# RWKV-7 chunk kernel with an MLP behind it: chunk operations in 64x64 tiles, PSUM banks in pairs, one full-array phase per slot

## The chip, the cores and the metric

The kernel runs on 1 core of one Trainium2 chip. The metric is the device time of one execution in microseconds, the median of three runs. Profiles are of one profiled execution. PE is TensorE, DVE VectorE, ACT ScalarE, POOL GpSimd, and SP the engine whose queue issues most DMAs.

## The reference

An RWKV-7 recurrence over 4 batch rows, 8 heads, 768 steps and a head size of 40, and then an MLP on each of the 3072 tokens:

```python
for t in range(S):
    y[:, :, t] = einsum('bhd,bhde->bhe', rt, state)
    Sa = einsum('bhde,bhe->bhd', state, at)
    state = state * wt[:, :, None, :] - einsum('bhd,bhe->bhde', Sa, bt)
    state = state + einsum('bhd,bhe->bhde', vt, kt)
x = y as (tokens, 320)
h = x @ w_in                                   # 320 -> 1024
solu = h * softmax(h)
ln = (solu - mean) / sqrt(var + 1e-6) * g_ln
out = ln @ w_out                               # 1024 -> 320, w_in, g_ln, w_out in float64
```

## The kernel before

The recurrence is worked in chunks of C = 64 steps. Two batch rows lie on the 128 partitions (64 steps each), so a *slot* i is one chunk of one pair of batch rows: 2 pairs times 12 chunks, N = 24 slots; the two pairs alternate, and the state `st` of a pair is carried from slot i to slot i + 2. A head's product is at most 64 by 64, and the array is used as four tiles of 64x64: `units` lists the 16 (p, g, q, h) of a slot (batch row p and head), and `in_turn` deals them out so that neighbouring instructions lie on different tiles. Other work uses the array as one: the transpositions of 128 rows (`turned`, four transposes of two heads each), the decay sums (`decay`: `pcum`, `pex`), the transposition of the MLP's activations (`folded`: `plnT`), and the two MLP products (`hidden`: `h`, `output`: `po`).

For a slot the steps are these. `load_keys` and `load_values` load w, b, k, a and v, r. `decay` takes the logarithm of w, sums it along time (`pcum`, `pex`), and scales b and k by the inverse decay (`kb`, POOL). `front` writes `kb` to DRAM and turns b and a (`pbT`, `paT`; `bT` is copied by ACT, `aT` is a product by `ex` on DVE). `norm` multiplies them (`pnt`), masks the product (`nt`) and writes it to DRAM. For each group of GRP = 4 slots `spread` gathers the 32x32 diagonal blocks of `nt` in `blk`, and `invert` inverts them on DVE, in 30 pairs of operations (`prod`, `uu`); they come back through DRAM by `bring` (`tu`, `uh`). `couple` and `close` (`py`, `pz`) make the off-diagonal part of the inverse. `fetch` brings `kb` back (`kbx`), `attend` turns k, v and r (`pkT`, `pvT`, `prT`), `states` turns the state (`psT`), `scores` multiplies (`ps`), `carried` and `driven` make the right side (`px`, copied to `x0`), `solved` applies the inverse (`pu`), `answered` (`pl`) and `read` (`pyo`) make the output and the new state, and `leave` scales both and sends the output to `xT`. Then come `hidden`, `weighed`, `spreadof`, `folded` and `output`, one and two slots later.

One Python loop over i from -9 to N + 1 writes all of this as a software pipeline: the step of slot i stands beside `norm` of slot j = i + 7 (AHEAD), `front` of j + 1, `decay` of j + 2 and `load_keys` of j + 3. PE's order is exactly the written one (`manual_schedule`); the orders of the other engines are set by the tile scheduler. `some(n)` takes the next n pairs of the inversion, `drawn(n)` the next n pieces of the weights' conversion from float64 (`narrow`, on DVE, POOL and ACT), which in the kernel before runs nine pieces at each of i = -4 to -1 and the rest at the end of i = 0. PSUM is one tag of six banks of 2 KB a partition (`bank`) and two banks for `h`. `in_value_order` copies v and r on POOL into another order of heads.

Of the kernel before, what the change touches and what calls it, by code (L numbers as in the profile page):

```python
# [45 lines left out]
def kernel(  # L46
# [34 lines left out]
    ps1 = ctx.enter_context(tc.tile_pool(name="ps1", bufs=6, space=PSUM))  # L81
# [32 lines left out]
    r_t = zeroed(nc.gpsimd, "r", [P, H, C], 2, pad)  # L114
    v_t = zeroed(nc.gpsimd, "v", [P, H, C], 2, pad)
# [12 lines left out]
    def bank(name):  # L128
        return ps1.tile([P, 512], FP32, tag="bank", name=name)
# [43 lines left out]
    def weights():  # L173
# [5 lines left out]
        pg = bank("pg")  # L179
# [6 lines left out]
        t = bank("pmean")  # L186
# [13 lines left out]
    units = [(p, g, q, h) for g in range(2) for p in range(2) for q in range(2) for h in range(2)]  # L200
# [16 lines left out]
    def pair(t, j):  # L217
        return t[:, j:j + 2, :].rearrange("p a b -> p (a b)")[:, 0:W2]
# [10 lines left out]
    def load(x, ap, i):  # L229
        bp, ci = where_(i)  # L230
        for p in range(2):
            nc.sync.dma_start(out=x[half(p), :, 0:D],
                              in_=ap[2 * bp + p, :, ci * C:(ci + 1) * C, :].rearrange("h t d -> t h d"))
# [5 lines left out]
    def load_keys(i):  # L239
        if not ok(i):  # L240
            return
        d = st[i]
        for n, ap in (("w", w), ("b", b), ("k", k), ("a", a)):
            x = a_t[i % 3] if n == "a" else two.tile([P, H, D], FP32, tag="raw_" + n, name="raw_" + n)
            d["raw_" + n] = x
            load(x, ap, i)

    def load_values(i):
        if not ok(i):
            return  # L250
        d = st[i]
        for n, ap in (("v", v), ("r", r)):
            d["raw_" + n] = two.tile([P, H, D], FP32, tag="raw_" + n, name="raw_" + n)
            load(d["raw_" + n], ap, i)

    def in_value_order(i):
        if not ok(i):
            return
        d = st[i]
        d["v"], d["r"] = v_t[i % 2], r_t[i % 2]  # L260
        d["lv"] = two.tile([P, H, W2], FP32, tag="lv", name="lv")
        for x, n in ((d["v"][:, :, 0:D], "raw_v"), (d["r"][:, :, 0:D], "raw_r"), (d["lv"][:, :, C:], "raw_v")):
            nc.gpsimd.tensor_copy(out=x.rearrange("p (h x) d -> p h x d", h=2),  # L263
                                  in_=d[n].rearrange("p (x h) d -> p h x d", h=2))


    def decay(i):
# [5 lines left out]
        t = bank("pcum")  # L273
        nc.tensor.matmul(heads(t[:, 0:DM]), lhsT=c_("cum"), rhs=lw[:, :, 0:D], start=True, stop=True)  # L274
        inv = two.tile([P, DM], FP32, tag="inv", name="inv", bufs=1)
        nc.scalar.activation(out=inv, in_=t[:, 0:DM], func=AF.Exp, scale=-1.0)  # L276
        t = bank("pex")
        for j in range(4):
            nc.tensor.matmul(t[0:W2, j * P:(j + 1) * P], lhsT=pair(lw, 2 * j), rhs=c_("cum"), start=True, stop=True)  # L279
        ex = d["ex"] = ex_t[i % (AHEAD + 3)]  # L280
        nc.scalar.activation(out=ex[0:W2, :, :, 1:].rearrange("p b j t -> p j b t"),
                             in_=t[0:W2].rearrange("p (j b t) -> p j b t", j=4, b=2), func=AF.Exp)
# [5 lines left out]
    def turned(name, src_, bufs=1, evict=True):  # L288
        t = bank("p" + name)
        for j in range(4):  # L290
            nc.tensor.transpose(out=t[0:W2, j * P:(j + 1) * P], in_=pair(src_, 2 * j), identity=ident)  # L291
        if not evict:
            return t
        o = two.tile([P, 4, P], FP32, tag=name, name=name, bufs=bufs)
        nc.scalar.copy(out=o[0:W2].rearrange("p j t -> p (j t)"), in_=t[0:W2])
        return o

    def front(i):
        if not ok(i):
            return  # L300
        d = st[i]
        nc.sync.dma_start(out=d["kb_dram"], in_=d["kbw"])
        ex = d["ex"]
        d["bT"] = turned("bT", d["kbw"][:, H:, :])
        t = turned("aT", d["raw_a"], evict=False)
        aT = d["aT"] = two.tile([P, 4, P], FP32, tag="aT", name="aT", bufs=AHEAD + 2)
        nc.vector.tensor_tensor(out=aT[0:W2].rearrange("p j (b t) -> p j b t", b=2),
                                in0=t[0:W2].rearrange("p (j b t) -> p j b t", j=4, b=2),
                                in1=ex[0:W2, :, :, 0:C].rearrange("p b j t -> p j b t"), op=ALU.mult)

    def masked(dst, t):
        nc.vector.tensor_tensor(out=dst, in0=t, in1=tri.unsqueeze(1).to_broadcast([P, 4, C]), op=ALU.mult)  # L312

    def keyed(t, i, u):
        p, g, q, h = u
        return t[rows(h), 2 * g + q, p * C:p * C + C]

    def valued(t, i, u):
        p, g, q, h = u
        return t[rows(q), 2 * h + g, p * C:p * C + C]  # L320

    def norm(i):
# [3 lines left out]
        t = [bank("pnt") for _ in range(2)]  # L326
        for u in in_turn(lambda p, g, q, h: (h, p ^ h)):
            p, g, q, h = u
            j = 2 * g + q
            mm(t[h][half(p ^ h), j * C:j * C + C], keyed(d["bT"], i, u), keyed(d["aT"], i, u))  # L330
        nt = d["nt"] = two.tile([P, 2, 4, C], FP32, tag="nt", name="nt", bufs=AHEAD + 1)
        for h in range(2):
            masked(nt[:, h], t[h][:, 0:256].rearrange("p (j c) -> p j c", j=4))
        d["nt_dram"] = dram.tile([P, H, C], FP32, tag="nt_dram", name="nt_dram", bufs=3)
# [35 lines left out]
    def bring(i):  # L370
# [6 lines left out]
        for x in range(2):  # L377
# [4 lines left out]
            nc.sync.dma_start(out=d["uh"][hi],  # L382
                              in_=uu[at + 16 + 8 * x:at + 24 + 8 * x, :, Q:].rearrange("h s t -> s h t"))

    def fetch(i):
# [3 lines left out]
        d["kb"] = two.tile([P, 2 * H, C], FP32, tag="kbx", name="kbx")  # L389
        nc.sync.dma_start(out=d["kb"], in_=d["kb_dram"])  # L390

    def couple(i):
# [3 lines left out]
        t = [bank("py") for _ in range(2)]  # L396
        for u in in_turn(lambda p, g, q, h: p ^ h):
            p, g, q, h = u
            j, x = 2 * g + q, half(p ^ h)
            mm(t[h][x, j * Q:j * Q + Q], d["nt"][x, h, j], d["tu"][x, 4 * h + j, 0:Q])  # L400
        for h in range(2):
            nc.scalar.activation(out=wy[:, h, :, 0:Q], in_=t[h][:, 0:4 * Q].rearrange("p (j c) -> p j c", j=4),
                                 func=AF.Copy, scale=c_("neg_hi"))

    def close(i):
# [3 lines left out]
        t = [bank("pz") for _ in range(2)]  # L409
        for u in in_turn(lambda p, g, q, h: p ^ h):  # L410
            p, g, q, h = u
            j, x = 2 * g + q, half(p ^ h)
            mm(t[h][x, j * Q:j * Q + Q], wy[x, h, j], d["uh"][x, 4 * h + j])
        for h in range(2):
            nc.scalar.copy(out=d["tu"][:, 4 * h:4 * h + 4, 2 * Q:], in_=t[h][:, 0:4 * Q].rearrange("p (j c) -> p j c", j=4))


    def attend(i):
# [3 lines left out]
        d["kT"] = turned("kT", d["kb"][:, 0:H, :])  # L422
        d["vT"] = turned("vT", d["v"])
        d["rT"] = turned("rT", d["r"], bufs=2)

    def scores(i):
# [3 lines left out]
        t = [bank("ps") for _ in range(2)]  # L430
        for u in in_turn(lambda p, g, q, h: (h, p)):
            p, g, q, h = u
            j = 2 * g + q
            mm(t[h][half(p), j * C:j * C + C], keyed(d["kT"], i, u), keyed(d["aT"], i, u))
        for u in in_turn(lambda p, g, q, h: (q, p)):
            p, g, q, h = u
            j = 4 + 2 * h + g
            mm(t[q][half(p), j * C:j * C + C], valued(d["vT"], i, u), valued(d["rT"], i, u))
        psi = d["psi"] = two.tile([P, 2, 4, C], FP32, tag="psi", name="psi")
        for x in range(2):  # L440
            masked(psi[:, x], t[x][:, 0:256].rearrange("p (j c) -> p j c", j=4))
        for x in range(2):
            masked(d["lv"][:, x::2, 0:C], t[x][:, 256:].rearrange("p (j c) -> p j c", j=4))


    def carried(i):
# [5 lines left out]
        d["px"] = [bank("px") for _ in range(2)]  # L452
        d["opened"] = set()
        if ci:
            for u in in_turn(lambda p, g, q, h: (h, p ^ h)):
                p, g, q, h = u
                j = 2 * g + q
                mm(d["px"][h][half(p ^ h), j * D:j * D + D], keyed(d["aT"], i, u),
                   st_t[bp][rows(h), 4 * p + j, 0:D], start=(h, p ^ h) not in d["opened"], stop=False)
                d["opened"].add((h, p ^ h))  # L460
            fence()

    def driven(i):
# [3 lines left out]
        for u in in_turn(lambda p, g, q, h: (p, p ^ h)):  # L467
            p, g, q, h = u
            j = 2 * g + q
            mm(d["px"][h][half(p ^ h), j * D:j * D + D], d["psi"][half(p), h, j],  # L470
               d["lv"][half(p), 4 * h + 2 * g + q, C:], start=(h, p ^ h) not in d["opened"])
            d["opened"].add((h, p ^ h))
        for h in range(2):
# [261 lines left out]
```

## Time and profile before

| | |
|---|---|
| median of 3 runs | 817.25 us (816.14 to 817.75) |
| the profiled execution | 821.3 us |
| its span | 819.5 us |
| mean granted TensorE clock | 0.863 of full speed |
| PE, DVE, ACT, POOL busy | 644.9, 379.0, 239.8, 168.4 us |
| DMA | 84.31 MB in 224901 packets |

The median is of plain runs; the profiled execution is 4 us longer. About 1.8 us of it lie outside the span. A row of the timeline gives the start, the duration, the engine and the line, the operation with its tiles (out<-in) and shapes, the number of instructions, and in brackets the idle time of the engine ahead of it with what ended it. A PE duration includes the pipeline's tail, so consecutive rows overlap, and the cost of a row is best read from start to start.

### The profile page before, as it was taken

To read this page: it belongs to the slowest core of one execution; us is meant where nothing else is said; L and a number is where in the kernel's file an instruction comes from. 1 tells how busy PE (TensorE), PEld (TensorE's weight loads), DVE (VectorE), ACT (ScalarE), POOL (GpSimd) and SP (SyncE) were. 2 spreads that over 40 slices of the span, in tenths; PEclk is the share of its full clock that TensorE was granted. 3 is DMA by queue.
4 is the path that set the end of the run, shared out by engine and by line. 5 is a ranking of instruction groups with operands and counts; after the bars stand their busy time and mean duration, and the time that the engine had idled before them with its cause. 6 is when DMAs were issued, how large, how long until landed. Compare 5 with 4: busy or idle time off the path is not lost.

```text
span 819.5 us, 26810 instructions
## 1 busy us (share of the span) xinstructions
PE 644.9 (79%) x11545; PEld 480.8 (59%) x11545; DVE 379.0 (46%) x1048; ACT 239.8 (29%) x592; POOL 168.4 (21%) x237
## 2 busy tenths in 40 slices
PE   4505506778989989889889899798997877989894
PEld 3304404657757766667667667676765665666652
DVE  3563572478403692343954228822479133123322
ACT  3323102323324322433234334133321222223121
POOL 6664234313202211221022102301111110000000
PEclk8655756669989989999989999799997789899997
DMA  7546847364464545554625655265422412011000
GB/s 149 145 133 138 204 109 191 64 138 95 96 169 108 111 79 129 155 122 89 146 80 115 152 133 127 49 161 125 97 70 52 120 47 54 23 52 41 15 20 13
DMA packets 224901, 84.31 MB, mean 103 GB/s; under 512 B 206088, under 2 KB 213136, under 8 KB 224016
## 3 DMA queue, kind: packets, MB, share of 16 engines
q1 hardware_dynamic: 220272, 76.12, 40.4%
q10 hardware_dynamic: 4512, 6.48, 2.7%
q8 instruction: 91, 1.49, 0.7%
q14 instruction: 26, 0.21, 0.1%
HBM read 49.53 MB, written 29.10 MB: 96 GB/s over the span
## 4 chain that ended last, share of the span: by engine, by line
PE 46%; DVE 23%; DMA 15%; issue 5%; POOL 5%; ACT 3%; SPq 2%; ACTq 0%; DVEq 0%; POOLq 0%
PE h L592 14%; PE po L642 10%; DMA kbx<-kb_dram 7%; DVE prod L360 5%; DVE uu L362 5%; PE pz L211 3%; PE pyo L211 3%; DVE e L604 3%; DVE nmax L595 3%; PE py L211 3%; DVE bs L612 2%; DMA uu_dram<-uu 2%; PE pu L211 2%; POOL n_s L143 2%; ACT e L598 2%
## 5 line engine op out<-in xcount | busy, mean ns | idle before, releaser
L595 DVE TENSOR_REDUCE nmax<-h 128x1 f32<-128x1024 f32 x24 | 29.4, 1223 | 305.0 <-PE h L592 305.0
L592 PE MATMUL h<-w_in,xT 120*128 120x512 f32 (+1 forms) x288 | 135.8, 622 | 0.0
L642 PE MATMUL po<-w,lnT 128*128 128x320 f32 x384 | 115.4, 456 | 3.9 <-ACT lnT L633 3.9
L642 PEld LDWEIGHTS po<-w,lnT 128*128 128x128 f32 x384 | 75.7, 203 | 34.9 <-ACT lnT L633 5.4
L592 PEld LDWEIGHTS h<-w_in,xT 120*128 120x128 f32 (+1 forms) x288 | 55.0, 197 | 62.2 <-issue 61.1
L598 ACT ACTIVATE e<-h,nmax 128x1024 f32<-128x1024 f32 x24 | 26.8, 1116 | 147.5 <-DVE nmax L595 147.5
L360 DVE TENSOR_TENSOR prod<-blk,uu 128x30 f32<-128x30 f32 (+9 forms) x180 | 62.9, 350 | 6.0
L362 DVE TENSOR_TENSOR uu<-uu,prod 128x30 f32<-128x30 f32 (+9 forms) x180 | 61.5, 342 | 5.7
L291 PE MATMUL pkT<-cst,kbx 128*104 128x128 f32 x96 | 18.7, 330 | 45.5 <-DMA kbx<-kb_dram 42.7
L621 POOL TENSOR_TENSOR rs<-c,mhalf 128x1 f32<-128x1 f32 x24 | 13.4, 557 | 188.7 <-DVE c L620 135.6
L285 POOL TENSOR_TENSOR kb<-raw_b,inv 128x320 f32<-128x320 f32 x24 | 20.9, 869 | 151.4 <-ACT inv L276 131.1
L291 PE MATMUL pbT<-cst,kb 128*104 128x128 f32 x96 | 18.4, 323 | 39.5 <-POOL kb L285 39.5
L263 POOL COPY v<-raw_v 128x320 f32<-128x320 f32 x24 | 10.9, 456 | 179.8 <-DMA raw_v<-in_v_dram 179.7
L274 PE MATMUL pcum<-lw,cst 128*128 128x320 f32 x48 | 24.6, 605 | 24.6 <-ACT lw L272 14.7
L211 PE MATMUL pyo<-lv,kbx 64*64 64x104 f32 x768 | 42.2, 268 | 0.5 <-DVE lv L312 0.4
L211 PE MATMUL pyo<-lu,kbx 64*64 64x104 f32 x768 | 41.0, 261 | 0.8 <-DVE lu L312 0.5
L291 PEld LDWEIGHTS pkT<-cst,kbx 128*104 128x104 f32 x96 | 12.2, 154 | 50.0 <-issue 46.9
L644 ACT ACTIVATE osb<-po,rs 128x320 f32<-128x320 f32 x24 | 12.7, 527 | 94.5 <-PE po L642 94.5
L211 PE MATMUL py<-tu,nt 64*64 64x32 f32 x768 | 30.6, 227 | 8.2 <-DMA tu<-uu_dram 6.0
L279 PEld LDWEIGHTS pex<-cst,lw 128*104 128x104 f32 x192 | 32.8, 223 | 7.0 <-issue 4.1
L474 ACT COPY x<-px 128x160 f32<-128x160 f32 x48 | 11.7, 295 | 83.7 <-PE plnT L632 25.4
L291 PEld LDWEIGHTS pbT<-cst,kb 128*104 128x104 f32 x96 | 11.4, 149 | 41.8 <-POOL kb L285 40.5
(105 smaller groups left out, 1253.1 us busy)
## 6 DMA issues: line engine op xcount, KB each, us to landing
kb_dram<-kb SPq DMA_DIRECT2D x24, 512.0 KB
kbx<-kb_dram SPq DMA_DIRECT2D x24, 512.0 KB
nt_dram<-nt SPq DMA_DIRECT2D x24, 256.0 KB
uu_dram<-uu SPq DMA_DIRECT2D x6, 1024.0 KB
raw_w<-in_w_dram SPq DMA_DIRECT2D x48, 80.0 KB
raw_b<-in_b_dram SPq DMA_DIRECT2D x48, 80.0 KB
raw_k<-in_k_dram SPq DMA_DIRECT2D x48, 80.0 KB
a<-in_a_dram SPq DMA_DIRECT2D x48, 80.0 KB
```

Source lines behind the costliest of these rows:

```text
L211: nc.tensor.matmul(o, lhsT=lhsT, rhs=rhs, start=start, stop=stop, skip_group_check=True)
L274: nc.tensor.matmul(heads(t[:, 0:DM]), lhsT=c_("cum"), rhs=lw[:, :, 0:D], start=True, stop=True)
L279: nc.tensor.matmul(t[0:W2, j * P:(j + 1) * P], lhsT=pair(lw, 2 * j), rhs=c_("cum"), start=True, stop=True)
L285: nc.gpsimd.tensor_tensor(out=kb[:, j * H:j * H + H, 0:D], in0=d["raw_" + n], in1=heads(inv), op=ALU.mult)
L291: nc.tensor.transpose(out=t[0:W2, j * P:(j + 1) * P], in_=pair(src_, 2 * j), identity=ident)
L360: nc.vector.tensor_tensor(out=t, in0=nb[:, j:j + 1, j + 1:Q].to_broadcast([P, j, m]), in1=u[:, 0:j, j:j + 1].to_broadcast([P, j, m]), op=A ...
L362: nc.vector.tensor_tensor(out=u[:, 0:j, j + 1:Q], in0=u[:, 0:j, j + 1:Q], in1=t, op=ALU.subtract)
L592: nc.tensor.matmul(h[:, hh], lhsT=d["xT"][0:n, kt, :], rhs=w_in[0:n, kt, hh], start=kt == 0, stop=kt == NK - 1)
L595: nc.vector.tensor_reduce(out=nmax, in_=h, axis=AX.X, op=ALU.max, negate=True)
L598: nc.scalar.activation(out=e, in_=h, func=AF.Exp, bias=nmax, accum_out=d["esum"])
L604: nc.vector.tensor_tensor(out=d["e"], in0=d["h"], in1=d["e"], op=ALU.mult)
L642: nc.tensor.matmul(o[:, 0:DM], lhsT=d["lnT"][:, f, :], rhs=w2[:, f, :], start=f == 0, stop=f == NF - 1)
```

## The change

- The transpositions of k, v, r, a, b and of the state become 16 pieces of 64x64 each (`turn`): a transpose where the result goes to the lower 64 partitions, a matmul by the identity where it goes to the upper ones. `pcum` becomes two products of 64x64 blocks, `pex` sixteen; `py` and `pz` go over four tiles in place of two.
- PSUM's six banks become three pairs (`banks`). k and v share a pair (`pkv`), r and the state another (`prs`), a and b a third (`pa`), the two halves of `plnT` a pair too. One operation evicts both banks: `x0`, `nuT`, `lu`, `wy`, `tu` on ACT, `nt`, `psi`, `lv`, `lu` on DVE.
- The heads keep their natural order: v and r are loaded straight to where they are used, and the POOL copies go. The state's update is two POOL operations in place of one.
- The loop's order: `attend`, `front` and `decay` stand ahead of `solved`; `folded`, `hidden` and `output` are consecutive; `answered`, `scores`, `read` follow. Drains stand ahead of `driven`'s products and ahead of the second half of `read`.
- `nt` is not kept but loaded again from DRAM in `fetch` (`ntx`); `kbx` has three buffers in place of two; `uh` comes in four loads in place of two; k and a of the first four slots are loaded by ACT's queue.
- The weights are converted at i = 0 (20 pieces) and i = 1 (the rest), none before.

```diff
-    def bank(name):
-        return ps1.tile([P, 512], FP32, tag="bank", name=name)
+    def banks(name):
+        return ps1.tile([P, 2, 512], FP32, tag="banks", name=name)
...
-    def turned(name, src_, bufs=1, evict=True):
-        t = bank("p" + name)
-        for j in range(4):
-            nc.tensor.transpose(out=t[0:W2, j * P:(j + 1) * P], in_=pair(src_, 2 * j), identity=ident)
-        if not evict:
-            return t
-        o = two.tile([P, 4, P], FP32, tag=name, name=name, bufs=bufs)
-        nc.scalar.copy(out=o[0:W2].rearrange("p j t -> p (j t)"), in_=t[0:W2])
+    def turn(t, to, of, at, x):
+        o, one = t[half(to), of, at:at + C], ident[half(of), half(of)]
+        if to:
+            mm(o, x, one)
+        else:
+            nc.tensor.transpose(out=o, in_=x, identity=one)
+
+    def turned(t, at, src_, keys):
+        for u in in_turn(lambda p, q, g, h: (p, h if keys else q)):
+            p, q, g, h = u
+            j = at + (2 * q + g if keys else 2 * g + h)
+            turn(t, h if keys else q, p, j * C, src_[half(p), head(u)])
+        return t[0:W2, :, at * C:at * C + 4 * C].rearrange("p b (j t) -> p b j t", j=4)
+
+    def kept(name, t, bufs=1):
+        o = tokens(name, bufs)
+        nc.scalar.copy(out=o[0:W2], in_=t)
         return o
...
     def front(i):
         nc.sync.dma_start(out=d["kb_dram"], in_=d["kbw"])
-        d["bT"] = turned("bT", d["kbw"][:, H:, :])
-        t = turned("aT", d["raw_a"], evict=False)
+        t = banks("pa")
+        a_ = turned(t, 0, d["raw_a"], True)
+        aT = d["aT"] = tokens("aT", AHEAD + 2)
+        nc.vector.tensor_tensor(out=aT[0:W2], in0=a_, in1=d["ex"][0:W2, :, :, 0:C], op=ALU.mult)
+        d["bT"] = kept("bT", turned(t, 4, d["kbw"][:, H:], True))
...
     def attend(i):
-        d["kT"] = turned("kT", d["kb"][:, 0:H, :])
-        d["vT"] = turned("vT", d["v"])
-        d["rT"] = turned("rT", d["r"], bufs=2)
+        t = banks("pkv")
+        d["kT"] = kept("kT", turned(t, 0, d["kb"], True))
+        d["vT"] = kept("vT", turned(t, 4, d["lv"][:, :, C:], False))
+        t = banks("prs")
+        d["rT"] = kept("rT", turned(t, 0, d["r"], False), 2)
+        if ci:
...
+                turn(t, q, h, at, st_t[bp][half(h), 4 * q + 2 * p + g])
+            d["s"] = kept("s", t[0:W2, :, 256:].rearrange("p h (j c) -> p h j c", j=4), 2)
...
     def folded(i):
+        t = banks("plnT")
         for x in range(2):
-            t = bank("plnT")
...
     def fetch(i):
-        d["kb"] = two.tile([P, 2 * H, C], FP32, tag="kbx", name="kbx")
+        d["kb"] = two.tile([P, 2 * H, C], FP32, tag="kbx", name="kbx", bufs=3)
         nc.sync.dma_start(out=d["kb"], in_=d["kb_dram"])
+        d["nt"] = tokens("ntx", 2)
+        nc.sync.dma_start(out=d["nt"].rearrange("p h j c -> p (h j) c"), in_=d["nt_dram"])
...
+        if i == 0:
+            drawn(20)
+        if i == 1:
+            drawn(100)
         carried(i)
         norm(j)
         driven(i)
...
-        in_value_order(i + 1)
-        folded(i - 2)
         attend(i + 1)
+        front(j + 1)
+        decay(j + 2)
         some(3)
         fetch(i + 2)
-        output(i - 2)
         solved(i)
         couple(i + 1)
         some(3)
+        folded(i - 2)
         hidden(i - 1)
-        answered(i)
         weighed(i - 1)
-        scores(i + 1)
+        output(i - 2)
         spreadof(i - 1)
         some(3)
-        front(j + 1)
-        decay(j + 2)
-        states(i + 1)
+        answered(i)
+        scores(i + 1)
         some(3)
-        if -4 <= i < 0:
-            drawn(9)
         read(i, True)
         close(i + 1)
         read(i, False)
         leave(i)
         if (i + 2) % GRP == 0:
             some(40)
-        if i == 0:
-            drawn(100)
         bring(i + 2)
```

## The prediction

> **What bounds the kernel now.** I read the page first, then the windows by stage, then PE's and ACT's timeline of one ordinary slot, then PE's in a late slot. The page gives busy time, the granted clock in 40 slices and the chain that ended last:
>
> ```profile
> PE 644.9 (79%) x11545; PEld 480.8 (59%) x11545; DVE 379.0 (46%) x1048; ACT 239.8 (29%) x592; POOL 168.4 (21%) x237
> PEclk8655756669989989999989999799997789899997
> PE 46%; DVE 23%; DMA 15%; issue 5%; POOL 5%; ACT 3%; SPq 2%; ACTq 0%; DVEq 0%; POOLq 0%
> ```
>
> PE carries the chain but is not the whole of it, and its clock is low for the first eight slices. The windows give, after the stretch, each engine's busy time (PE first) and then the clock:
>
> ```profile
> 0.00:93.00 93.00, 38.94 (x310) 30.55 (x310) 43.60 (x130) 27.47 (x62) 50.01 (x63) 0.63 0.65 150
> 93.00:166.00 73.00, 37.06 (x593) 29.40 (x597) 38.39 (x97) 15.97 (x40) 26.64 (x30) 0.65 0.56 130
> 373.00:482.00 109.00, 97.86 (x1943) 73.64 (x1944) 55.09 (x154) 37.04 (x92) 19.10 (x29) 0.97 0.53 119
> ```
>
> So 166 us pass before slot 1 opens (93 to the first inversion) with PE under half busy. From there four slots take about 109 us, PE 90% busy, clock 0.97. One ordinary slot on PE (start, duration with the pipeline's tail, idle before it in brackets):
>
> ```profile
> 475.23 1.09 PE L632 MATMUL plnT<-cst,e 128*128 128x128 f32 x8
> 476.84 0.62 PE L291 MATMUL pkT<-cst,kbx 128*104 128x128 f32 x4 [0.52 <-DMA kbx<-kb_dram]
> 477.29 0.60 PE L291 MATMUL pvT<-cst,v 128*104 128x128 f32 x4
> 477.73 0.60 PE L291 MATMUL prT<-cst,r 128*104 128x128 f32 x4
> 478.16 4.47 PE L642 MATMUL po<-w,lnT 128*128 128x320 f32 x16
> 482.56 0.69 PE L211 MATMUL pu<-tu,x 64*64 64x64 f32 x32
> 483.52 1.11 PE L211 MATMUL py<-tu,nt 64*64 64x32 f32 x32
> 496.43 1.07 PE L211 MATMUL pz<-uh,wy 64*64 64x32 f32 x28 [0.22 <-DVE c L618]
> ```
>
> Three groups of transpositions run back to back, 0.44 us each, because each has its own bank. Their evictions on ACT trail behind and nobody on PE waits for them:
>
> ```profile
> 477.54 0.59 ACT L295 COPY kT<-pkT 104x512 f32<-104x512 f32 x1 [0.50 <-PE pkT L291]
> 478.02 0.59 ACT L295 COPY vT<-pvT 104x512 f32<-104x512 f32 x1
> 478.50 0.60 ACT L295 COPY rT<-prT 104x512 f32<-104x512 f32 x1
> ```
>
> Late slots instead wait for kbx, and the work after the wait runs at half speed (pkT 1.07 us for 0.62, po 6.02 for 4.47):
>
> ```profile
> 635.51 1.97 PE L632 MATMUL plnT<-cst,e 128*128 128x128 f32 x8
> 639.70 1.07 PE L291 MATMUL pkT<-cst,kbx 128*104 128x128 f32 x4 [2.22 <-DMA kbx<-kb_dram]
> 642.27 6.02 PE L642 MATMUL po<-w,lnT 128*128 128x320 f32 x16
> ```
>
> The sum is made against the profiled execution, 821.3 us (span 819.5 and 1.8 outside). The median is 817.25, so a sum is brought to it by 0.995.
>
> **PE work that goes.** A 64x64 transposition group becomes 8 transposes into columns 0 and 8 matmuls by the identity into columns 64 (two instructions each): 24 instructions over four tiles. Rows of 32 such instructions over four tiles take 0.45 to 0.53 us (pu above to its next group at 483.08: 0.52), so I take 0.45 for a group of 24, as now (0.44): no gain. The bounds are 0.38 and 0.9, the latter if the transposes and the matmuls don't overlap. py and pz use two tiles (1.04 and 1.07 us for 32); over four I take 0.5, the price of the other groups of 32: -1.1. pcum with pex (0.54 and 0.88) become about 1.0: -0.4. The kbx wait of 0.52 goes, since kbx gets a third buffer: -0.5. Two waits of 0.38 and 0.22 ahead of the reading-out are covered by the new order: -0.6. Together -2.6 us in an ordinary slot of 25.3 (px 472.73 to px 498.05).
>
> The phases of full-array work fall from three to one. Between rows I see no stop worth more than 0.1: the last h to pl is 5.36 us for 12 matmuls at 0.443, and the second ps to pbT is 0.58 for its own 0.47. I take 0; the other bound is four changes by 0.11 by 24 slots, -10 us. The Trainium skill, "TensorEngine Tiling (Array Packing)", Key Properties, says that changing the tiling mode drains TensorE, which speaks for the change; it gives no price, and at the row's 0.11 us it is that bound.
>
> **New waits on PE.** Two banks are now one tile, and PE's order is fixed. In the built order the transposes of v, which write the same pair as those of k, wait for ACT's copy of kT; those of st for the copy of rT; those of kb for DVE's aT multiply; the second half of plnT for the first lnT copy. Price of one from the rows: group start to copy start 0.70 (476.84 to 477.54), copy 0.59, start of the next 0.1: 1.39 instead of 0.44, so +0.95. With ACT's x0 copy (0.45) ahead of kT it is 1.15; st 1.1; kb with aT's 0.68 on DVE 1.05; plnT, whose copy stands behind nuT, lu and wy on ACT, 1.4 (0.4 if the scheduler's order let it go first). Together +4.7. Behind each waiting instruction stands all of PE, po and h too. The ordinary slot becomes 25.3 - 2.6 + 4.7 = 27.4 us.
>
> **By groups.** A group from pu to pu is now 25.2, 31.1, 26.1 and 27.1 (109.5). The two long ones after the inversion hold kbx waits, so they become 27.4 as well: +2.2, +1.3, +0.3. The inversion slot changes most in one place: 24 inversion operations (8.2 us by their rows, 390.88 to 399.06) now stand on DVE before aT, and PE's kb transposes wait for it, some 3.4 us later than in other slots; h comes that much later, so nmax, which now waits behind 34 inversion operations, waits less. I take +1.7. That is +5.5 a group, three groups +16.5; slots 13 to 16 +4.7 (105.9 before). From slot 17 on there is no front or decay left: 27.4 less pa, its wait, pb and the decays (3.0) is 24.4, and the kbx waits of 4 to 5 us with their half clock go: slots 17 to 20 take 107 for 117.4, -10.4, and the last ones -3. Sum from slot 1 on: +8, with bounds -30 (half the new waits hidden) and +20.
>
> SP gets a load of nt and two more of uh in each slot, about 1.3 us by their rows; it is done 5 us before its next slot now, which covers them. POOL loses three copies of 0.45, off the path.
>
> **Prologue.** No weight is narrowed before slot 0 any more (nine pieces at each of four steps before), and a norm step takes about 7 us for 8.9, with k and a of the first slots on ACT's queue. The first inversion then starts at 44 to 50 instead of 93. But the narrowing (20 pieces, about 3 us each by POOL's 1.2 to 1.3 and 0.7 to 1.1 a piece and the hops) falls behind it and holds slot 0's and slot 1's evictions and pmean: slot 1 opens near 149, for 166. -17, bounds -30 and +5.
>
> **The clock.** From S+2.85 to S+8 of the new slot (S its px) PE works 1.8 of 5.1 us, in pieces of 0.45. Before's trace shows what idle time does: 1.71 us idle ahead of the plnT at 198.42 was followed by half speed until 201.77; waits of 2 to 3.6 us in inversion and late slots by 4 to 8 us of it; while stretches with up to 43% of 3.4 us idle (the slots at 340 and 367) kept full speed. The new stretch has 65% idle in its worst 3.4 us. Half speed from about S+6.5 to past pu and py would double up to 3 us of PE work. I charge 2.2 us in 12 of 23 slots, +26, with bounds 0 and +60 (2.6 in every slot). The Trainium skill, "TensorE: Matmul & The Clock Gate", Part 1, lets the clock fall after an idle window of some 3.4 us: by that alone none of these stretches counts and the charge is 0, but the row at 198.42 fell after less. Its Part 4 holds that transposes don't count as busy in the same way, by which every slot would fall: +60.
>
> Sum: 821.3 + 8 - 17 + 26 = 838; by 0.995, **834 us**.
>
> **Rivals.** *The clock holds* (faster): the pieces between the waits are enough to keep full speed, as with the 43% windows. 821.3 + 8 - 17 = 812, median 808, and 785 to 812 with the drains saved or waits shorter. It decides at 9 us: fewer than 4 slots charged. For it: the pieces are never more than 1.15 us apart. Against it: 198.42. Chance 0.36. *Transposes and identity matmuls don't share the array* (slower): 0.9 instead of 0.45 us for six groups in 23 slots, +62 less what the waits take up, 860 to 890; no row mixes the two. 0.12. *My forecast, false waits plus the clock*: 0.49, alone 818 to 865. *Nothing measurable*, prologue and waits cancelling: 0.03; 0.2% is about what can be told from no change.
>
> The range takes the faster case from 790 and the slower one up to 880. Faster 0.37, same 0.03, slower 0.60.
>
> **What would show it.** Right: pkv's second half, prs's second, pa's second and plnT's second each with 1 to 1.5 us idle released by ACT kT, rT, DVE aT, ACT lnT; ordinary slots 27 to 30 us; PEclk below 0.9 in the slices from 160 to 590 that read 9 now; kbx gone from the waits; late slots near 24.5; slot 1 at 140 to 155. Wrong: four slots in under 110 us at full clock, a transposition group over 0.7 us at full clock, or slot 1 after 166.

## The result and the profile after

The changed kernel takes 1413.38 us (median of 4 runs, 1408.09 to 1417.93), 1.729 times the kernel before (95% interval 1.722 to 1.736). The forecast was 834 us. Its profiled execution spans 1409.7 us. The page's busy times, the granted clock by slices, and the chain that ended last:

```profile
PE 1210.4 (86%) x15009; PEld 822.3 (58%) x15009; DVE 369.3 (26%) x882; ACT 239.1 (17%) x472; POOL 143.7 (10%) x189
PEclk9655555567577576675775765766756777767779
PE 80%; issue 6%; ACT 4%; DVE 3%; POOL 3%; DMA 2%; ACTq 0%; SPq 0%; DVEq 0%; POOLq 0%
PE pa L211 10%; PE pkv L211 10%; PE h L589 9%; PE prs L211 8%; PE po L639 7%; PE pa L287 6%; PE pkv L287 6%; PE prs L287 5%; PE pyo L211 3%; PE pu L211 3%; PE px L211 2%; PE plnT L629 2%; PE pcum L211 2%; PE ps L211 2%; POOL n_s L143 1%
```

PE's busy time has nearly doubled (644.9 before), and 45% of the span lies on the chain in pa, pkv and prs, the transpositions, which were cheap before. The clock is never back at 9 in the steady part. PE's timeline of one group shows how (L287 is a transpose, L211 the matmul by the identity, two instructions):

```profile
807.42 0.31 PE L287 MATMUL prs<-cst,r 64*64 64x64 f32 x1
807.66 0.47 PE L211 MATMUL prs<-cst,r 64*64 64x64 f32 x2
808.06 0.31 PE L287 MATMUL prs<-cst,r 64*64 64x64 f32 x1
808.30 0.47 PE L211 MATMUL prs<-cst,r 64*64 64x64 f32 x2
...
812.16 0.47 PE L211 MATMUL prs<-cst,r 64*64 64x64 f32 x2
813.40 0.31 PE L287 MATMUL prs<-cst,st 64*64 64x64 f32 x2 [0.77 <-ACT rT L302]
813.64 0.48 PE L211 MATMUL prs<-cst,st 64*64 64x64 f32 x4
814.05 0.32 PE L287 MATMUL prs<-cst,st 64*64 64x64 f32 x2
814.30 0.48 PE L211 MATMUL prs<-cst,st 64*64 64x64 f32 x4
```

Read from start to start. A matmul begins 0.24 us after the transpose ahead of it, and the next transpose 0.24 us after that matmul's second instruction; no other piece starts in between, and no semaphore is waited for. In the state's group, from 813.40 on, two transposes start within 0.01 us of each other, and so do the matmuls behind them: work of one kind does run side by side. The order there is T T M M where the others have T M T M, so it has 8 changes of kind in place of 16, and it takes 2.68 us where the others take 5.2 (medians over the slots). That is 0.33 us a change in either, with the work itself.

The clock follows the groups. In one slot it is full over the MLP and the reading-out, and half over the transpositions, though PE is 92% busy there (stretch, its length, PE, PEld, DVE, ACT, POOL, then the clock):

```profile
774.00:794.00 20.00, 16.96 (x361) 11.79 (x358) 7.72 (x15) 4.81 (x10) 1.42 (x3) 1.00 0.18 62
797.00:827.00 30.00, 27.72 (x148) 17.62 (x149) 0.69 (x1) 2.34 (x4) 0.00 (x0) 0.50 0.41 88
```

The predicted waits are there too, each in nearly every slot (total, times, longest):

```profile
PE pkv L287 <- ACT kT L302: 23.8, 24, 5.6
PE pa L287 <- DVE aT L313: 20.2, 24, 0.9
PE plnT L629 <- ACT lnT L630: 19.7, 24, 1.2
PE prs L287 <- ACT rT L302: 16.8, 22, 0.8
```

They are 80 us of the 590 by which the span grew, and cannot be the cause alone.

### The profile page after: what moved, and what is told of

Its sections match the earlier page's. It is cut to its first block, busy times and chain, and to the rows that moved or that the text cites. A ratio compares the mean times of both kernels' runs of the same rounds, so it can differ in the third digit from the quotient of the medians.

```text
span 1409.7 us, 33414 instructions
## 1 busy us (share of the span) xinstructions
PE 1210.4 (86%) x15009; PEld 822.3 (58%) x15009; DVE 369.3 (26%) x882; ACT 239.1 (17%) x472; POOL 143.7 (10%) x189
## 3 DMA queue, kind: packets, MB, share of 16 engines
q1 hardware_dynamic: 216048, 81.11, 23.6%
## 4 chain that ended last, share of the span: by engine, by line
PE 80%; issue 6%; ACT 4%; DVE 3%; POOL 3%; DMA 2%; ACTq 0%; SPq 0%; DVEq 0%; POOLq 0%
PE pa L211 10%; PE pkv L211 10%; PE h L589 9%; PE prs L211 8%; PE po L639 7%; PE pa L287 6%; PE pkv L287 6%; PE prs L287 5%; PE pyo L211 3%; PE pu L211 3%; PE px L211 2%; PE plnT L629 2%; PE pcum L211 2%; PE ps L211 2%; POOL n_s L143 1%
## 5 line engine op out<-in xcount | busy, mean ns | idle before, releaser
L211 PE MATMUL pkv<-cst,lv 64*64 64x64 f32 x384 | 90.7, 337 | 0.0
L211 PE MATMUL prs<-cst,r 64*64 64x64 f32 x384 | 90.7, 337 | 0.0
L211 PE MATMUL pa<-cst,kb 64*64 64x64 f32 x384 | 90.2, 337 | 0.0
L211 PE MATMUL pa<-cst,a 64*64 64x64 f32 x384 | 89.2, 333 | 0.0
L211 PE MATMUL pkv<-cst,kbx 64*64 64x64 f32 x384 | 85.0, 319 | 0.4 <-issue 0.4
L287 PE MATMUL pkv<-cst,lv 64*64 64x64 f32 x192 | 59.5, 310 | 23.8 <-ACT kT L302 23.8
L287 PE MATMUL pa<-cst,kb 64*64 64x64 f32 x192 | 59.2, 308 | 20.2 <-DVE aT L313 20.2
L287 PE MATMUL pkv<-cst,kbx 64*64 64x64 f32 x192 | 56.7, 295 | 21.1 <-DMA kbx<-kb_dram 19.8
L211 PEld LDWEIGHTS prs<-cst,r 64*64 64x64 f32 x384 | 54.7, 202 | 22.2
L211 PEld LDWEIGHTS pkv<-cst,lv 64*64 64x64 f32 x384 | 54.7, 202 | 22.2
L211 PEld LDWEIGHTS pa<-cst,kb 64*64 64x64 f32 x384 | 54.1, 199 | 22.2
L211 PEld LDWEIGHTS pa<-cst,a 64*64 64x64 f32 x384 | 53.4, 197 | 21.8
L211 PEld LDWEIGHTS pkv<-cst,kbx 64*64 64x64 f32 x384 | 50.6, 186 | 20.6 <-issue 0.5
```

The source lines that it names most:

```text
L211: nc.tensor.matmul(o, lhsT=lhsT, rhs=rhs, start=start, stop=stop, skip_group_check=True)
L287: nc.tensor.transpose(out=o, in_=x, identity=one)
```

## The experiments

**Theory A**: at each change between transposing and multiplying PE waits until the work before it is done. **Rival B**: small pieces of either kind run one at a time. **Rival C**: the prediction's own cause, shared bank pairs and the clock. The first three runs vary only the kind and order of the pieces.

All pieces by matmul:

```diff
-        if to:
-            mm(o, x, one)
-        else:
-            nc.tensor.transpose(out=o, in_=x, identity=one)
+        mm(o, x, one)
```

> Every 64x64 piece of a transposition is a matmul by the identity; none is a transpose. Theory A (each change between transposing and multiplying waits until the array is empty, 0.24 us at half clock, 16 changes a group): a group falls from 5.2 to about 0.5 us, a slot from 55 to 27-30 us, the total to 800-840 us. Rival B (small pieces of either kind run one at a time): 16 matmuls by 0.40 us, 6.4 us a group, the total at 1450 us or more. Rival C (the shared bank pairs and the clock that falls behind them are the cause): the clock stays near 0.68 and the total above 1200 us.

Measured: 905.93 us (896.1 to 906.74), 1.099 of before (1.090 to 1.109). Order, tiles and banks are as in the changed kernel, so they are not the cause. B falls, and C as the main cause: the clock rises to 0.80 and the total is far under 1200. A holds for the 507 us that went, but not for the total of 800 to 840: 85 us are left over the kernel before.

The transposes of a group first, then the matmuls:

```diff
-        for u in in_turn(lambda p, q, g, h: (p, h if keys else q)):
+        lot = in_turn(lambda p, q, g, h: (p, h if keys else q))
+        for u in sorted(lot, key=lambda u: u[3] if keys else u[1]):
...
-            for u in in_turn(lambda p, q, g, h: (h, q)):
+            for u in sorted(in_turn(lambda p, q, g, h: (h, q)), key=lambda u: u[1]):
```

> The same pieces as in the changed kernel, but in each group the 8 transposes come first and then the 8 matmuls: one change inside a group and one between groups in place of 16. Theory A: a group of 0.7 to 1.0 us, the total at 830-890 us. Rival B: 8 x 0.31 us and more remain for the transposes, a group of 3 us or more, the total above 1100 us. Rival C: no change, near 1413 us.

Measured: 960.75 us (957.54 to 966.19). A group takes 1.68 us at half speed, above A's 0.7 to 1.0, and about 1.0 at its fastest. The total is 70 us above A's 890, about what the run before had left over.

T T M M in place of T M T M:

```diff
+        lot = in_turn(lambda p, q, g, h: (p, h if keys else q))
+        for u in [lot[n + k] for n in range(0, 16, 4) for k in (0, 2, 1, 3)]:
```

> Pieces in the order T T M M in place of T M T M, as the state's group already has them: 8 changes a group in place of 16. Theory A: each of five groups falls from 5.2 to 2.7 us, 12.6 us a slot, the total to about 1413 - 24 x 12.6 = 1110 us (somewhat lower with the prologue). Rivals B and C: near 1413 us.

Measured: 1131.22 us (two runs, 1124.55 and 1137.90), all groups 2.3 to 2.7 us. The same pieces, the same banks and the same waits, and half the changes take 282 us off.

The fewer the changes of kind, the shorter the slot. Changes a slot, against the mean of 12 slots from slot 2 on (px to px):

| kernel | changes a slot | us a slot |
|---|---|---|
| changed kernel | 5 x 16 + 8 = 88 | 55.9 |
| T T M M | 6 x 8 = 48 | 42.6 |
| transposes first | 6 x 2 = 12 | 35.8 |
| all matmuls | 0 | 32.3 |
| kernel before | 0 | 27.9 |

From row to row a change costs 0.33, 0.19 and 0.29 us; over all, 23.6 / 88 = 0.27. These prices hold the change of clock as well. No run shows why a change costs this: the trace gives each piece's 64x64 shape, not the mode in which the array runs it.

k, a and b by four transposes of the full array, v, r and the state by matmuls:

```diff
-        if to:
-            mm(o, x, one)
-        else:
-            nc.tensor.transpose(out=o, in_=x, identity=one)
+        mm(o, x, one)
...
     def turned(t, at, src_, keys):
+        if keys:
+            o = t[:, at // 4]
+            for j in range(4):
+                nc.tensor.transpose(out=o[0:W2, j * P:(j + 1) * P], in_=pair(src_, 2 * j), identity=ident)
+            return o[0:W2].rearrange("p (j b t) -> p b j t", j=4, b=2)
```

> k, a and b are turned by four transposes of the full array each, as in the kernel before; v, r and the state by matmuls with the identity. Theory A: the groups of k, a, b cost 0.44 us and what a change of mode costs beside it, the total within 15 us of the run where all pieces are matmuls (800-850 us). If a change between full-array and tiled work costs as much as one between transposing and multiplying (0.12 us at full clock), four more changes a slot add about 0.5 us a slot, 12 us. Rival B: v, r and the state stay at 6.4 us each, the total above 1100 us.

Measured: 894.29 us (880.80 to 899.19), 12 below the run of all matmuls and within the 15 us of A; by the two quickest of its four runs, 887, it is 19 below. B falls. Changing between whole groups of full-array and tiled work costs nothing that this shows, but 2016 PE instructions went with it, and what they saved could hide a small price.

What is left, 85 us, is a second question. In the run of all matmuls PE's timeline reads:

```profile
535.25 1.13 PE L211 MATMUL pkv<-cst,lv 64*64 64x64 f32 x32 [0.73 <-ACT kT L299]
536.15 1.08 PE L211 MATMUL prs<-cst,r 64*64 64x64 f32 x32
538.03 1.13 PE L211 MATMUL prs<-cst,st 64*64 64x64 f32 x32 [0.80 <-ACT rT L299]
538.91 1.10 PE L211 MATMUL pa<-cst,a 64*64 64x64 f32 x32
540.82 1.13 PE L211 MATMUL pa<-cst,kb 64*64 64x64 f32 x32 [0.81 <-DVE aT L310]
...
546.90 0.66 PE L626 MATMUL plnT<-cst,e 128*128 128x128 f32 x4 [0.91 <-ACT lnT L627]
```

These are the four waits of the prediction, with the groups between them at half speed: 1.13 us for 32 instructions that take 0.68 elsewhere. **Theory D** says that these hold the rest; **rival E**, from idle gaps in the same timeline that no semaphore ends, that PE runs out of instructions. **Theory F** puts a part on the weights' new place.

Waits covered, all pieces still by matmul: `attend` and `front` now turn k, r and a only, `attend_b` and `front_b` v, the state and b, and the halves of plnT stand on both sides of the solve (the loop's part of the edit):

```diff
         attend(i + 1)
         front(j + 1)
+        attend_b(i + 1)
+        front_b(j + 1)
         decay(j + 2)
...
+        folded(i - 2, 0)
         solved(i)
         couple(i + 1)
-        folded(i - 2)
+        folded(i - 2, 1)
```

> As the run with all pieces as matmuls, but the groups are ordered so that no group follows the one whose eviction it waits for: k, r, a, then v, the state, b; and the first half of the activations' transposition is put ahead of the solve, the second behind it. Theory D (the waits on shared bank pairs, about 4 us a slot, and the clock that falls behind them hold most of the 66 us from slot 1 on): the four waits shrink from 0.7-0.9 us each to under 0.3, the clock rises from 0.80 to 0.87 or more, the total to 845-865 us. Rival E (PE's instruction supply: 16145 instructions in place of 11545, with idle gaps that no semaphore ends, about 1.6 us a slot against 0.15 before): the waits go but the gaps stay or grow, the total at 875-900 us.

Measured: 837.14 us, 1.023 of before (1.019 to 1.027). D holds, with 69 us: the waits on lnT and rT are all but gone (1.5 and 0.3 us), those on kT and aT left in 5 and 8 places, and the total is below D's 845 to 865. The clock, 0.848, is short of the 0.87 that D asked, and E's gaps grew. PE's timeline of this run, where "issue" is a gap that no semaphore ends:

```profile
472.46 0.58 PE L211 MATMUL pnt<-aT,bT 40*64 40x64 f32 x24 [0.73 <-issue]
473.18 0.68 PE L211 MATMUL px<-lv,psi 64*64 64x40 f32 x32
473.66 0.68 PE L211 MATMUL pkv<-cst,kbx 64*64 64x64 f32 x32
474.16 0.65 PE L211 MATMUL prs<-cst,r 64*64 64x64 f32 x32
474.62 0.30 PE L211 MATMUL pa<-cst,a 64*64 64x64 f32 x6
476.51 0.62 PE L211 MATMUL pa<-cst,a 64*64 64x64 f32 x26 [1.58 <-issue]
476.91 0.68 PE L211 MATMUL pkv<-cst,lv 64*64 64x64 f32 x32
477.38 0.68 PE L211 MATMUL prs<-cst,st 64*64 64x64 f32 x32
477.91 0.69 PE L211 MATMUL pa<-cst,kb 64*64 64x64 f32 x32
478.43 0.72 PE L211 MATMUL pcum<-lw,cst 64*64 64x320 f32 x4
478.97 0.22 PE L211 MATMUL pex<-cst,lw 64*64 64x64 f32 x1
481.06 0.69 PE L211 MATMUL pex<-cst,lw 64*64 64x64 f32 x31 [1.87 <-issue]
```

The gaps stop PE in the middle of a group of equal instructions; in these lines they lie 126 and 127 matmuls apart. From 200 to 760 us there are 54 of them here, 52.9 us in all, against 9 and 3.1 us in the kernel before; 51 of the 54 end 1.2 to 1.9 us after a 16 KB transfer of the instruction queue has ended. There are 100 such transfers in these 560 us, so by chance about one gap in eight would.

The weights converted early, as before, in the run of all matmuls (the rest of them at the end of i = 0):

```diff
-        if i == 0:
-            drawn(20)
-        if i == 1:
-            drawn(100)
...
+        if -4 <= i < 0:
+            drawn(9)
         read(i, True)
...
+        if i == 0:
+            drawn(100)
         bring(i + 2)
```

> As the run with all pieces as matmuls, but the weights are converted where the kernel before has it: nine pieces at each of i = -4 to -1, the rest at the end of i = 0. Theory F (converting them at i = 0 and 1 holds slot 1 back, 192.8 us to its solve for 174.4 before): the solve of slot 1 comes at 165-180 us and the total falls by 15-25 us to 880-892. Rival (the early conversion only moves the same work and delays the first inversion): the total within 8 us of 906.

Measured: 897.26 us, 9 less, below the 15 to 25 expected and just past the rival's 8; the times overlap (890.0 to 898.2, and 896.1 to 906.7 without it). Slot 1's solve comes at 190.1 us and not at 165 to 180, and the first inversion starts at 97.7 us for 62.6 without the edit: the work was moved, as the rival says. F is not shown to be more than a few us.

All mends at once (the edits above together), and the same without the early weights:

> The three mends together with fewer instructions: k, a, b by four full-array transposes each, v, r and the state by matmuls, the waits covered as in e5, the weights early as in e6. Theories D and F together: 894 less 45 and less 20, 825-840 us. Rival E: as fewer instructions are issued here (three groups of 4 for 32), the gaps without a semaphore are fewer than in e5, and this run lies more than 25 us under e5 even after the weights' 20.

Measured: 810.74 us, 0.993 of before (0.989 to 0.996), below the 825 to 840 of D and F, and 26 us below the run with the waits covered.

> As e5 (waits covered, weights late), but k, a, b by four full-array transposes each: 14129 PE instructions in place of 16145. Rival E, instruction supply: in e5 the idle gaps on PE that no semaphore ends sum to 52.9 us between 200 and 760 us, and nearly all end 1.3 to 1.5 us after a 16 KB transfer of the instruction queue; with an eighth fewer instructions the sum falls to about 30-35 us and the total by 10-20 us to 817-827 us. If the gaps have another cause, or full-array groups among tiled ones cost a change of mode each (4 more changes by 0.1 us and 24 slots), the total stays at 832-845 us.

Measured: 814.56 us, 0.998 of before (0.995 to 1.001). With k, a and b at 4 instructions for 32, the gaps sum to 31.1 us for 52.9 and the total falls by 22.6: E holds, at the size of the gaps. The groups' own work explains little of it, since at full clock a group takes 0.50 us as 32 matmuls and 0.44 as 4 transposes, about 4 us in all. But it was the number of instructions that was changed, not their supply alone. The early weights are then worth 4 us (810.74 for 814.56).

The third buffer of kbx alone, in the kernel before. `nt`, read again, has two buffers for eight here and eleven places in DRAM for three, which the lines below leave out:

```diff
-        d["kb"] = two.tile([P, 2 * H, C], FP32, tag="kbx", name="kbx")
+        d["kb"] = two.tile([P, 2 * H, C], FP32, tag="kbx", name="kbx", bufs=3)
         nc.sync.dma_start(out=d["kb"], in_=d["kb_dram"])
+        d["nt"] = two.tile([P, 2, 4, C], FP32, tag="ntx", name="ntx")
+        nc.sync.dma_start(out=d["nt"].rearrange("p h j c -> p (h j) c"), in_=d["nt_dram"])
```

> The kernel before with one part of the change alone: a third buffer for kbx, and nt read again from DRAM, which makes room for it. If the kbx waits on PE (42.7 us in 17 slots in the profile before, with half clock behind the long ones) come from the shared buffer, they go and the total is 775-800 us. Rival (kbx is late for its place on SP's queue and not for its buffer): within 5 us of the kernel before.

Measured: **785.32 us, 0.960 of before (0.955 to 0.965)**, the fastest kernel here. Of the kbx waits on PE one is left, ahead of slot 0, and the late slots (the last seven) take 23.0 us for 26.5. The clock reads 9 in nearly every slice from the eleventh on. In the kernel before, the load of kbx (L390) waited on SP's queue for `pyo`, the last reader of the old buffer, 17 times; here it does so once, for 7.9 us. So the rival falls. The clock and the wait of this run, then SP's wait before:

```profile
PEclk9655656588999998999999999999999899999997
PE pkT L291 <- DMA kbx<-kb_dram: 13.0, 1, 13.0
SPq L390 <- PE pyo L211: 137.8, 17, 12.9
```

The whole change with its mends, 810.74 us, holds this buffer too, and still stands 25 us above it.

The same with py and pz over four tiles (py's part of the edit):

```diff
-        for u in in_turn(lambda p, g, q, h: p ^ h):
+        for u in in_turn(lambda p, g, q, h: (p ^ h, p)):
...
-            mm(t[h][x, j * Q:j * Q + Q], d["nt"][x, h, j], d["tu"][x, 4 * h + j, 0:Q])
+            mm(t[h][half(p), j * Q:j * Q + Q], d["nt"][x, h, j], d["tu"][x, 4 * h + j, 0:Q])
```

> The kernel before with two parts of the change: the third buffer for kbx with nt read again (as in e7, 785 us), and py and pz over four tiles in place of two. By the rows of before each falls from 1.05 to 0.5 us, on PE's path in every slot: 24 x 1.1 = 26 us, so 757-765 us. Rival: the two extra loads of uh on SP, or ACT's wy and tu copies behind py and pz, set the slot's end, and the total stays at 778-788 us.

Measured: 787.25 us (779.12 to 789.55), no gain; the rival's 778 to 788 holds as a number. py does fall near the price from the rows:

```profile
452.85 0.67 PE L211 MATMUL py<-tu,ntx 64*64 64x32 f32 x32
453.45 5.42 PE L596 MATMUL h<-w_in,xT 120*128 120x512 f32 x12
```

py takes 0.60 us start to start, for 1.04 in the run before it. From slot 1's px to slot 23's, py and pz together take 18.9 us less on PE, but the stretch is only 0.8 us shorter: PE's idle time there grows by 12.5 us (45.9 to 58.4), and its other work takes 5.5 us more, at a clock of 0.952 for 0.961. The gaps without a semaphore grow by 5.7 us and the waits on the loads of `tu` and kbx by 7.2, while the others shrink a little. Why they grow stays open.

## Why the prediction was wrong

**The step that failed** is the price of a transposition group: "I take 0.45 for a group of 24 ... The bounds are 0.38 and 0.9". It measured 5.2 us at half clock. The 0.45 came from rows of 32 instructions that were all matmuls; no row of before mixed transposes and matmuls, and the bound was set as if each kind took its own turn once, in a block. For that case it is near: with the transposes first a group takes about 1.0 us at its fastest. As built, each of 16 changes takes 0.24 us from start to start. A slot takes 55.9 us where 27.4 were forecast, and 23.6 of the difference go when no group mixes the two kinds. The rival "transposes and identity matmuls don't share the array" named the place, had 0.12, and was mis-sized for the same reason, 62 us for 507.

**The drains.** The prediction counted four changes of phase saved at 0 to 0.11 us each, and weighed the Trainium skill's "Mode switching requires drain" ("TensorEngine Tiling (Array Packing)", Key Properties) only on that side. The run with full-array keys shows no price for such changes. That sentence of the page speaks of the tiling mode; what the trace shows is a price of 0.24 us from start to start at each change of kind, with all pieces of 64x64. Whether the transposes run in another tiling mode than the matmuls, so that this is the page's drain, no run shows.

**Waits and clock** were right in kind. Four waits of 0.7 to 0.9 us stand where they were put, shorter than the 1 to 1.5 forecast; the groups between them ran at half clock in the run of all matmuls, and that run's slots took 32.3 us where 27 to 30 were said. Covering the waits gave 2.8 us a slot in the 12 slots of the table (32.33 to 29.56). So the direction, slower, had a sound reason; the size came from the step above. In the changed kernel itself the clock is lower still, and not for idle time: it is 0.50 where PE is 92% busy with transpositions. Over several slots that gives, with PE 90% busy, a mean of 0.69. The cause of this is not shown beyond the rows.

```profile
480.00:700.00 220.00, 197.70 (x2526) 135.18 (x2524) 55.13 (x126) 36.45 (x71) 15.08 (x21) 0.69 0.26 61
```

**The prologue** was wrong in sign. The first inversion was to start at 44 to 50 us; it starts at 105.5 in the changed kernel and at 62.6 in the run of all matmuls, for 93.0 before. Even there slot 1's solve comes at 192.8 us, 18 later than before (174.4), where 17 earlier was forecast. The early weights don't change this (190.1); what holds it back stays open.

**kbx** was right: one wait is left of 17, and the buffer is worth 33 us without the rest of the change. The sum for the late slots has a slip: four slots of 24.4 are 97.6 us and not 107, which would put the forecast some 9 us lower and changes nothing in the account. **py and pz** were right as rows (0.6 us) and wrong as a gain.

**Missing altogether** was the supply of instructions. The all-matmul form has 4600 more matmuls; its gaps sum to 27.5 us, and to 52.9 once the waits are covered, for 3.1 in the same stretch of the kernel before.

## What to carry to other kernels

Price a mix by a row that mixes: before transposes and matmuls are interleaved on tiles, count the changes of kind, and put equal kinds together or use one kind. When an edit splits work into more, smaller instructions, look for idle gaps inside groups of equal instructions that no semaphore ends, beside the instruction queue's transfers. And try the parts of a large change one by one: here a third buffer for kbx, with `nt` read again, held the gain (0.960) that the rest of the change buried.

## What the runs showed of the hardware

- At a change between an fp32 transpose and an fp32 matmul of 64x64 the next piece starts 0.24 us later at half clock; in slot time a change cost 0.27 us. Two transposes on two tiles start within 0.01 us of each other.
- PE that is shown 92% busy but alternates in this way was granted a clock of 0.50 (797 to 827 us of the changed kernel), against 0.97 at 90% busy before (373 to 482 us).
- In the run with the waits covered, 51 of 54 of PE's gaps without a semaphore end 1.2 to 1.9 us after a 16 KB transfer of the instruction queue; two neighbouring spans between gaps hold 126 and 127 matmuls.
